# Attention, a gated layer and a soft mixture of experts on one core: sums joined on VectorE, more additions on VectorE, new due times, PSUM pairs in three pools, weights moved by 96 bytes

## The chip, the cores and the metric

The program runs on one core of a Trainium2 chip, as one launch. The metric is the device time of an execution in microseconds (us). A core has five engines that run their own instruction queues and meet at semaphores: PE (TensorE, matrix products into PSUM), DVE (VectorE), ACT (ScalarE), POOL (GpSimd), and SP (SyncE), which here issues all DMAs. A queue is executed in order: an instruction that waits holds up all that stand behind it.

## The reference

```python
def _attn_ref(q, k, v):                       # (4, 8, 1152, 64) each, fp32
    q_pool = q.reshape(B, H, S // 2, 2, D).mean(axis=3)
    scores = matmul(q_pool, k.transpose(0, 1, 3, 2)) / sqrt(D)
    scores = scores - max(scores, axis=-1)
    attn = exp(scores)
    attn = attn / (sum(attn, axis=-1) + 1e-09)
    return matmul(attn, v)

x = attention, laid out as (2304, 512)
h = x @ w_in                                  # (512, 2048)
x = (h * cos(h)) @ w_out                      # (2048, 512)

logits = x @ phi                              # 32 slots, 8 experts of 4 slots
slot_input = softmax(logits, over tokens).T @ x
slot_out[e] = relu(slot_input[e] @ w1[e]) @ w2[e]
return softmax(logits, over slots) @ slot_out
```

## The kernel before

**Three stages** follow one another: attention (up to about 416 us of the profiled execution), the gated layer (to about 790 us), the experts and the output (to the end). The change is in attention, in the passage to the gated layer, and in where the gated layer's weights lie.

**Attention** runs over 16 pairs of heads. A pair has 576 pooled queries in two halves of 288, and such a half is called a unit here: 32 units of J = 9 steps, one step for 128 keys. A step is: `scores` on PE (L347 four fp32 products, which the trace shows as eight; L351 four bf16 products that subtract the maximum), `exp` on ACT (L356), `av` on PE (L364, the product with v into the tile `o`), and `add` (L374), which adds the step's exponentials to a partial sum, on POOL or on DVE by the string `ADD_BY`. Before, "GGVGGVGGV" gives six steps to POOL (five additions) and three to DVE (two additions). After the ninth step `finish` multiplies the partial sums by ones on PE (`sums`, L431), which sums over the keys: one pass for the partial sum of POOL, one for that of DVE. Then `sums_out` on ACT (L438), four small DMAs (`fold`, L445), `total` on POOL (L449), `inv` on DVE (L453), DMAs `row` (L458) and `spread` (L462), `scale` on POOL (L465), and `store`, the split of the result into a high and a low part on ACT (L479) and POOL (L477). `take` (ACT, L417) and `join` (DVE, L421) read `o`.

**The maximum** of a pair's scores is found ahead of it: 14 rounds of a bf16 product on PE (`round_`, L274), each with a maximum over 768 columns on DVE (`reduce`, L279); `by_head` (PE, L286), `top` (DVE, L293 and L298) and `diagonal` (ACT, L305) make of them the tile D that L351 uses.

**PSUM** has 16 KB a partition. Attention uses three pairs of banks of 4 KB (`BANKS`, tags s0 to s2 of one pool `a_ps`) for scores, rounds and sums alike, and a fourth for `o`. The gated layer's pools `ps_h` and `ps_o` take over that memory.

**The order** is made by the class `Plan`. Every operation has an engine, a time that it is thought to take, what it follows, the ring buffers that it takes, and a due time. `Plan.order` goes forward in planned time and takes the operation that can start first; among those of one engine that can start at once, it takes the one that is due first. The plan lets no operation of POOL run beside an operation of DVE that is marked `port`. The due times are multiples of P, the planned time of a step. The instructions are then written out in that order, with semaphores from the data; nothing waits for a planned time.

**The gated layer** has 8 chunks of 256 of the 2048 columns, and 5 blocks of tokens (four of 512, one of 256). `gate` makes a product with w_in (L684, named hps), then its cosine in turns of ACT and DVE (L699 to L719) and a low part on POOL (L722); `project` multiplies with w_out (L684, named ops). Each product is three of fp32r: high by high, high by low, low by high. The first block of the first chunk (`first_gates`) is still planned with attention and takes one of its three PSUM pairs. The weights w come as 64-bit numbers and are decoded (L620 to L650) into high and low tiles: for even chunks into the pool `wts0`, which is allocated from the right end of SBUF, for odd chunks into `wts1i` and `wts1o` on the left. As built, the tiles of `wts0` start at bytes such as 202,720, which is 32 past a multiple of 64; those of `wts1i` and `wts1o` start at multiples of 128.

## Time and profile before

| | us |
|---|---|
| three runs | 918.54, 914.24, 917.77 (median 917.77) |
| the profiled execution | 914.82 |
| its span, first to last instruction | 912.9 |
| to the first scores | 17.9 |
| pairs 0 to 14, from the first scores of each | 374.5 |
| the last pair, to its last product in a row | 23.5 |
| from there to the second block's products in a steady row | 23.4 |
| gated layer to 790 us | 350.7 |
| the rest | 122.1 |

The page of the profile gives busy time and counts per engine, 40 slices of the span, the chain of work that ended last, and the costliest groups. The rows further down come from it and from answers of the trace. In a row by line and shape stand: line, engine, operation, output<-inputs, shapes, count | busy us, mean ns of one | idle time of the engine just before, with what ended it. A row of the timeline has the start, the time from start to end, and the instruction; "x8" is a run of eight. The time of one instruction on DVE or ACT includes the tail in which its writes land, and the next instruction can start inside it.

### The profile page before, as it was taken

How to read it: one execution, taken by the hardware profiler on the slowest of the kernel's cores; microseconds unless marked ns; L12 is line 12 of the kernel's file. 1: busy time of each engine (PE TensorE's matmuls, PEld its weight loads, DVE VectorE, ACT ScalarE, POOL GpSimd, SP SyncE). 2: the span in 40 equal slices, each digit the busy share in tenths (PEclk: the TensorE clock that was granted, in tenths of full speed). 3: DMA queues.
4: the chain of work that ended last, by engine and by line, in shares of the span. 5: the costliest groups of instructions: out<-in, count | busy, mean ns of one | idle time of the engine just before them, and what ended most of it. 6: DMA issues, size and time to landing. Idle time of an engine off the chain costs nothing.

```text
span 912.9 us, 24964 instructions
## 1 busy us (share of the span) xinstructions
PE 877.0 (96%) x10181; PEld 650.7 (71%) x10181; DVE 691.0 (76%) x1261; ACT 546.9 (60%) x1150; POOL 455.0 (50%) x445
## 2 busy tenths in 40 slices
PE   5999999899999999997999999999999999999997
PEld 2667766666666656765888888888888888777555
DVE  5778888787887878743899998888989887545524
ACT  3777777677777766674686554555555555445224
POOL 0677777776877767785444334334333343211000
PEclk9999999999999999998999999999999999999998
DMA  4133232333333332112111111111111110754797
GB/s 156 57 109 105 70 110 76 103 97 110 108 96 83 94 109 91 46 20 54 49 51 47 47 45 36 36 47 39 57 35 47 36 47 12 320 233 185 281 420 246
DMA packets 61363, 91.53 MB, mean 100 GB/s; under 512 B 29120, under 2 KB 40896, under 8 KB 57152
## 3 DMA queue, kind: packets, MB, share of 16 engines
q1 hardware_dynamic: 61248, 89.93, 30.5%
q8 instruction: 80, 1.31, 0.6%
q14 instruction: 35, 0.29, 0.1%
HBM read 78.71 MB, written 4.72 MB: 91 GB/s over the span
## 4 chain that ended last, share of the span: by engine, by line
PE 85%; DVE 5%; DMA 3%; ACT 3%; SPq 1%; issue 1%; POOL 0%; DVEq 0%; ACTq 0%; POOLq 0%
PE hps L684 21%; PE ops L684 20%; PE s L347 13%; PE o L364 13%; PE s L351 3%; PE m L274 3%; PE sums L431 3%; DVE mp L279 2%; PE hq L1225 2%; PE so L1268 2%; DVE r L702 1%; DMA kr<-in_k_dram 1%; DMA r<-row 1%; ACT r L709 1%; DMA qr<-in_q_dram 1%
## 5 line engine op out<-in xcount | busy, mean ns | idle before, releaser
L279 DVE TENSOR_REDUCE mp<-m 128x2 f32<-128x768 f32 x224 | 211.3, 951 | 56.8 <-PE m L274 56.2
L356 ACT ACTIVATE e<-s 128x576 f32<-128x576 f32 x288 | 184.1, 650 | 82.9 <-PE s L351 78.3
L684 PE MATMUL hps<-x,w 128*128 128x512 f32 (+1 forms) x960 | 211.9, 375 | 6.3 <-DVE r L712 6.3
L374 POOL TENSOR_TENSOR acc<-acc,e 128x576 f32<-128x576 f32 x128 | 185.4, 1449 | 64.0 <-ACT e L356 61.6
L684 PE MATMUL ops<-w,g 128*128 128x512 f32 x864 | 206.7, 393 | 0.0
L684 PEld LDWEIGHTS hps<-x,w 128*128 128x128 f32 x960 | 169.5, 190 | 41.8 <-DVE r L712 6.8
L347 PE MATMUL s<-qs,kr 64*64 64x288 f32 x2304 | 196.6, 408 | 2.8 <-ACT e L356 1.7
L364 PE MATMUL o<-e,vr 64*64 64x288 f32 x2304 | 190.1, 403 | 0.0
L684 PEld LDWEIGHTS ops<-w,g 128*128 128x128 f32 x864 | 161.5, 188 | 36.5 <-issue 0.6
L722 POOL TENSOR_TENSOR g<-r,g 128x512 fp32r<-128x512 f32 (+1 forms) x80 | 100.6, 1258 | 156.4 <-ACT g L719 120.7
L709 ACT ACTIVATE r<-r 128x512 f32<-128x512 f32 (+1 forms) x160 | 94.0, 587 | 76.2 <-DVE r L702 74.7
L347 PEld LDWEIGHTS s<-qs,kr 64*64 64x64 f32 x2304 | 89.5, 134 | 42.9 <-ACT e L356 4.8
L647 POOL TENSOR_TENSOR da<-da,w 128x256 f32<-128x256 f32 x64 | 51.1, 799 | 104.9 <-DVE db L636 43.6
L364 PEld LDWEIGHTS o<-e,vr 64*64 64x64 f32 x2304 | 87.4, 133 | 20.7
L274 PE MATMUL m<-kb,qb 64*64 64x384 bf16 x896 | 81.0, 335 | 14.1 <-ACT kb L234 5.7
L351 PE MATMUL s<-D,a_ones 64*64 64x288 bf16 x1152 | 90.7, 284 | 0.0
L702 DVE SCALAR_TENSOR_TENSOR r<-ki,hps 128x512 f32<-128x512 int32 (+1 forms) x80 | 50.3, 629 | 40.1 <-ACT ki L699 38.2
L699 ACT ACTIVATE ki<-hps 128x512 int32<-128x512 f32 (+1 forms) x80 | 44.1, 551 | 50.9 <-PE hps L684 50.6
L719 ACT CAST g<-r 128x512 fp32r<-128x512 f32 (+1 forms) x80 | 46.1, 577 | 41.4 <-DVE r L712 41.3
L374 POOL TENSOR_TENSOR acc<-e 128x576 f32<-128x576 f32 x32 | 46.5, 1455 | 44.1 <-ACT e L356 43.6
L835 DVE TENSOR_TENSOR acc<-acc,ops 128x512 f32<-128x512 f32 x70 | 47.3, 682 | 21.3 <-PE ops L684 21.2
L274 PEld LDWEIGHTS <-qb 64*64 64x64 bf16 x896 | 32.4, 108 | 39.2 <-issue 10.9
(146 smaller groups left out, 1005.4 us busy)
## 6 DMA issues: line engine op xcount, KB each, us to landing
raw<-in_w_io_dram SPq DMA_DIRECT2D x64, 256.0 KB
w1t<-in_w_dram SPq DMA_DIRECT2D x15, 1024.0 KB
vr<-in_v_dram SPq DMA_DIRECT2D x16, 576.0 KB
qr<-in_q_dram SPq DMA_DIRECT2D x15, 576.0 KB
kr<-in_k_dram SPq DMA_DIRECT2D x15, 576.0 KB
w2t<-in_w2b_dram SPq DMA_DIRECT2D x8, 1024.0 KB
r<-row SPq DMA_DIRECT2D x32, 144.0 KB
late<-in_w2a_dram SPq DMA_DIRECT2D x4, 1024.0 KB
```

Of the source, the lines that this page charges most:

```text
L274: nc.tensor.matmul(ps[heads[c], h.start // 64, 0:self.KC], w, m, start=True, stop=True)
L279: nc.vector.tensor_reduce(out=self.mp[p][:, x], in_=st[i][:, :, 0:self.KC], axis=AX.X, op=ALU.max)
L347: nc.tensor.matmul(ps[y:y + 64, h, 0:N], w, self.qs[p][x, s], start=True, stop=False)
L351: nc.tensor.matmul(ps[y:y + 64, h, 0:N], self.ones16[x], D[x, s], start=False, stop=True)
L356: nc.scalar.activation(out=st["e"], in_=st["ps"][:, :, 0:N], func=ACTF.Exp, scale=1.0 / 16.0)
L364: nc.tensor.matmul(self.o[u][64 * h:64 * h + 64, r, 0:N], self.vr[p][x, h, t], st["e"][x, h], start=(t == 0), stop=(t == J - 1),)
L374: eng.tensor_tensor(out=acc[who], in0=x, in1=st["e"], op=ALU.add)
L647: nc.gpsimd.tensor_tensor(out=st["a"], in0=st["a"], in1=fl(half(0)), op=ALU.subtract)
L684: nc.tensor.matmul(ps, x, y, start=(i == 0 and m == 0), stop=(i == n - 1 and m == 2))
L702: nc.vector.scalar_tensor_tensor(out=st["r"], in0=st["ki"], scalar=-c, in1=x, op0=ALU.mult, op1=ALU.add)
L709: nc.scalar.activation(out=st["r"], in_=st["r"], **kw)
L722: nc.gpsimd.tensor_tensor(out=g["l"][:, i], in0=st["r"], in1=fl(g["h"][:, i]), op=ALU.subtract)
```

## The change

1. `JOIN_BY = "V"`: DVE adds its partial sum to POOL's (`join_sums`, 128 x 2 x 288 fp32), and `sums` is one pass over one operand where it was two.
2. `ADD_BY` is "VVVVGGGGV": four additions on DVE and three on POOL in a unit, where it was two and five. `scale` and the low part of `store` stay on POOL.
3. The due times of attention become a table `DUES` with new values, with new values of P, `ROUNDS`, `BEHIND` and the first weights' times; the times in which loads are thought to land are longer; the first gates follow the decoding of the first weights. Only the order on the engines comes from these.
4. The three PSUM pairs become three pools of one buffer, and they are placed by which pair is used last, the earliest at the bottom.
5. A tile `edge` of 96 bytes is allocated at the right end ahead of `dec` and `wts0`. The tiles of `wts0` then start at 202,624 and the like, multiples of 128.
6. `consts` is written under the hand-made order as well.

```diff
-    P = 1.31
+    P = 1.3
-    ADD_BY = "GGVGGVGGV"
+    ADD_BY = "VVVVGGGGV"
-    BEHIND = 3.5
+    BEHIND = 6.36
+    DUES = {
+        "load": -0.1, "free": 4.8, "v": 10.9, "pooled": -16.1, "qb": 9.0, "kb": -8.9, "top": -21.5,
...
+    JOIN_BY, SCALE_BY, LOW_BY = "V", "G", "G"
+    HOLD = 3
...
-        self.ps_s = pool("a_ps", 1, space=PSUM)
+        self.ps_s = [pool(f"a_ps{i}", 1, space=PSUM) for i in range(self.BANKS)]
...
     def bank(self, key, name):
-        i = self.plan.slot[key]
-        return self.ps_s.tile([128, 2, 512], FP32, tag=f"s{i}", name=name)
+        return self.ps_s[self.place[self.plan.slot[key]]].tile([128, 2, 512], FP32, tag="s", name=name)
...
+        def join_sums():
+            self.engine(self.JOIN_BY).tensor_tensor(out=acc["G"], in0=acc["G"], in1=acc["V"], op=ALU.add)
+            del acc["V"]
...
-            x = op(s + 2 * P, who, (0.667, 1.37)[who == "G"],
+            x = op(s + due["add"] * P, who, (0.667, 1.37)[who == "G"],
...
+        if self.JOIN_BY:
+            x = op(s + due["whole"] * P, self.JOIN_BY, (0.667, 1.37)[self.JOIN_BY == "G"], join_sums,
+                   [where["G"][2], where["V"][2]], uses=[("aG", u), ("aV", u)], port=True)
+            where = {"G": (0, 0, x)}
         self.finish(p, c, avs[-1], [(x, (f"a{who}", u)) for who, (_, _, x) in where.items()] + whole, acc)
...
-        t = op(s + 3 * P, "P", 0.485 * len(adds), sums, [i for i, _ in adds], new=[("s", self.BANKS, ("sums", u))],
+        t = op(due("sums"), "P", 0.485 * len(adds), sums, [i for i, _ in adds], new=[("s", self.BANKS, ("sums", u))],
...
+        left = {}
+        for key, slot in plan.slot.items():
+            if plan.sizes_of[key] == "s":
+                left[slot] = max(left.get(slot, 0.0), *(start[i] for i in plan.users[key]))
+        self.place = {x: i for i, x in enumerate(sorted(left, key=left.get))}
...
-FIRST_FROM, FIRST_EVERY = 2, 1.6
+FIRST_FROM, FIRST_EVERY, FIRST_DUE = 2.68, 1.75, 159.1
...
+    edge = pool(ctx, "edge", 1, side="right").tile([128, 24], FP32, name="edge")
+    nc.vector.memset(edge, 0.0)
...
-            x = last[-2:] + done[:1]
+            x = last[-2:] + decoded + done[:1]
```

**VectorE in the middle of attention.** The rows are about one unit in the sixth pair before (mp<-m is a maximum, acc an addition of exponentials, mc the top, fold the inverse, xu the joining of `o`):

```order
L279 TENSOR_REDUCE mp<-m 128x2
L374 TENSOR_TENSOR acc<-e 128x576
L279 TENSOR_REDUCE mp<-m 128x2
L453 RECIPROCAL fold<-fold 128x36
L279 TENSOR_REDUCE mp<-m 128x2 x2
L421 TENSOR_TENSOR xu<-xu,o 128x288
L279 TENSOR_REDUCE mp<-m 128x2 x2
L374 TENSOR_TENSOR acc<-acc,e 128x576
L293 TENSOR_REDUCE mc<-m 128x4
```

And after, one unit at the like place (acc<-acc is the joining of the partial sums; da is a piece of the decoding):

```order
L388 TENSOR_TENSOR acc<-acc,e 128x576
L443 TENSOR_TENSOR xu<-xu,o 128x288
L391 TENSOR_TENSOR acc<-acc 128x576
L657 TENSOR_SCALAR da<-da 128x256
L388 TENSOR_TENSOR acc<-e 128x576
L660 TENSOR_SCALAR da<-da 128x256
L388 TENSOR_TENSOR acc<-acc,e 128x576
L665 SCALAR_TENSOR_TENSOR da<-raw,da 128x256
L388 TENSOR_TENSOR acc<-acc,e 128x576
L294 TENSOR_REDUCE mp<-m 128x2 x2
L475 RECIPROCAL fold<-fold 128x36
L294 TENSOR_REDUCE mp<-m 128x2 x2
```

Before, the additions stand singly between maxima; after, the unit's last addition, the joining and three additions of the next unit stand together, and the maxima follow together.

**ScalarE at the same places**, where e<-s is the exponential of a step. Before:

```order
L356 ACTIVATE e<-s 128x576 x2
L438 ACTIVATE r_3412<-sums 128x576
L305 ACTIVATE D<-a_minus,mc 128x64 x5
L356 ACTIVATE e<-s 128x576 x2
L479 CAST x_68<-xu 128x160
L479 CAST x_70<-xu 128x128
L644 CAST w<-da 128x256
L234 CAST qb<-qs 128x576
L356 ACTIVATE e<-s 128x576
L234 CAST kb<-kr 128x384
```

After:

```order
L320 ACTIVATE D<-a_minus,mc 128x64 x4
L460 ACTIVATE r_3266<-sums 128x576
L439 COPY xu<-o 128x288
L371 ACTIVATE e<-s 128x576 x8
L503 CAST x_68<-xu 128x288
L371 ACTIVATE e<-s 128x576
L320 ACTIVATE D<-a_minus,mc 128x64 x5
```

The exponentials of a unit, spread between other work before, now follow one another, seven or eight in a row; on PE the scores do so too, seven steps of a unit in a row ahead of its first product with v.

**TensorE at the end of attention**, with what a row waits for (hps<-x_66 is the first block's gate product, hps<-x_68 the second block's). Before:

```order
L684 MATMUL hps<-x_66,w 128x512
L431 MATMUL sums<-acc,a_ones 64x288 [waits PE_49,Pool_49]
L431 MATMUL sums<-acc,a_ones 64x288 x3
L431 MATMUL sums<-acc,a_ones 64x288 [waits DVE_49]
L431 MATMUL sums<-acc,a_ones 64x288 x3
L364 MATMUL o<-e,vr 64x288 [waits Activation_49]
L364 MATMUL o<-e,vr 64x288 x3
L684 MATMUL hps<-x_68,w 128x512 [waits DVE_49]
L684 MATMUL hps<-x_69,w 128x512
```

After:

```order
L379 MATMUL o<-e,vr 64x288 x4
L453 MATMUL sums<-acc,a_ones 64x288 [waits PE_49]
L453 MATMUL sums<-acc,a_ones 64x288 x3
L379 MATMUL o<-e,vr 64x288 x12
L453 MATMUL sums<-acc,a_ones 64x288 [waits DVE_49,PE_49]
L453 MATMUL sums<-acc,a_ones 64x288 x3
L720 MATMUL hps<-x_68,w 128x512 [waits Activation_49]
L720 MATMUL hps<-x_69,w 128x512 [waits Pool_49]
```

The second block's product waited for the last DVE instruction that reads the first block's products, since both lay in the lowest pair of banks; after, the first block's products lie in the highest of the three pairs, and the second block's first product waits for the ACT instruction that reads the sums of the last unit but one. The sums of the last two units stand close together there, and two gate products of the first block lie between products with v.

## Rows read from the trace of the kernel before

**Rows 1.** The page: busy by engine; the chain that ended last; exponentials.

```profile
PE 877.0 (96%) x10181; PEld 650.7 (71%) x10181; DVE 691.0 (76%) x1261; ACT 546.9 (60%) x1150; POOL 455.0 (50%) x445
...
PE 85%; DVE 5%; DMA 3%; ACT 3%; SPq 1%; issue 1%; POOL 0%; DVEq 0%; ACTq 0%; POOLq 0%
...
L356 ACT ACTIVATE e<-s 128x576 f32<-128x576 f32 x288 | 184.1, 650 | 82.9 <-PE s L351 78.3
```

**Rows 2.** Windows: length, busy of PE, PEld, DVE, ACT, POOL, clock, DMA, GB/s.

```profile
17.90:392.40 374.50, 365.90 (x6908) 253.28 (x6912) 300.13 (x433) 270.14 (x578) 276.87 (x253) 1.00 0.31 90
392.40:415.90 23.50, 23.50 (x440) 15.30 (x432) 10.62 (x15) 16.29 (x31) 19.52 (x19) 1.00 0.14 31
415.90:439.30 23.40, 17.14 (x83) 12.87 (x80) 9.29 (x19) 10.04 (x23) 8.78 (x11) 0.85 0.17 39
439.30:790.00 350.70, 350.70 (x1601) 289.13 (x1600) 306.48 (x650) 199.48 (x411) 136.75 (x145) 1.00 0.17 51
```

**Rows 3.** Groups by line and shape in 17.9 to 392.4 us.

```profile
L431 PE MATMUL sums<-acc,a_ones 64*64 64x288 f32 x464 | 33.9, 406 | 2.5 <-ACT e L356 1.4 <-DVE mp L279 0.8
...
L279 DVE TENSOR_REDUCE mp<-m 128x2 f32<-128x768 f32 x208 | 196.8, 951 | 55.1 <-PE m L274 54.5
L374 DVE TENSOR_TENSOR acc<-e 128x576 f32<-128x576 f32 x30 | 27.7, 924 | 0.3 <-ACT e L356 0.3
L374 DVE TENSOR_TENSOR acc<-acc,e 128x576 f32<-128x576 f32 x29 | 25.5, 881 | 0.0
...
L374 POOL TENSOR_TENSOR acc<-acc,e 128x576 f32<-128x576 f32 x119 | 172.2, 1447 | 60.7 <-ACT e L356 58.5
L374 POOL TENSOR_TENSOR acc<-e 128x576 f32<-128x576 f32 x30 | 43.7, 1458 | 43.9 <-ACT e L356 43.6
```

**Rows 4.** The chain of work in order of time, 405 to 450 us: start, length.

```profile
407.51 0.97 PE sums L431 x16
408.48 0.48 PE s L347 x8
408.97 0.12 PE s L351 x4
409.09 0.48 PE o L364 x8
```

**Rows 5.** Timeline of DVE and POOL: start, length, instruction.

```profile
8.98 7.01 DVE L279 TENSOR_REDUCE mp<-m 128x2 f32<-128x768 f32 x8
...
195.64 0.75 DVE L374 TENSOR_TENSOR acc<-acc,e 128x576 f32<-128x576 f32 x1
196.31 0.95 DVE L279 TENSOR_REDUCE mp<-m 128x2 f32<-128x768 f32 x1
...
414.94 1.41 POOL L374 TENSOR_TENSOR acc<-acc,e 128x576 f32<-128x576 f32 x1
...
415.34 1.63 DVE L374 TENSOR_TENSOR acc<-acc,e 128x576 f32<-128x576 f32 x1
```

**Rows 6.** The chain as in Rows 4, 180 to 192 us: a round.

```profile
188.35 0.16 PE m L274 x4
```

**Rows 7.** Timeline of PE at the end of attention.

```profile
421.75 1.20 PE L431 MATMUL sums<-acc,a_ones 64*64 64x288 f32 x16
422.77 0.66 PE L364 MATMUL o<-e,vr 64*64 64x288 f32 x8
429.70 8.33 PE L684 MATMUL hps<-x,w 128*128 128x512 f32 x24 [6.26 <-DVE r L712]
```

**Rows 8.** A window there, columns as in Rows 2.

```profile
429.70:435.10 5.40, 5.40 (x13) 4.24 (x14) 0.38 (x1) 0.60 (x1) 1.52 (x2) 0.50 0.11 20
```

**Rows 9.** Groups by shape on PE, weights of chunk 2: from 516.9 and 556.0 us.

```profile
L684 PE MATMUL hps<-x,w 128*128 128x512 f32 x24 | 5.8, 396 | 0.0
...
L684 PE MATMUL ops<-w,g 128*128 128x512 f32 x24 | 5.8, 396 | 0.0
```

**Rows 10.** The same, weights of chunk 1: from 489.5 and 494.9 us.

```profile
L684 PE MATMUL hps<-x,w 128*128 128x512 f32 x24 | 5.6, 389 | 0.0
...
L684 PE MATMUL ops<-w,g 128*128 128x512 f32 x24 | 5.6, 389 | 0.0
```

More of the change, by code (lines that the diff above doesn't have):

```diff
@@ L122 @@
 class Attention:
-    P = 1.31
+    P = 1.3
     QB, KC = 64, 384
-    ADD_BY = "GGVGGVGGV"
-    ROUNDS = (-13, -12, -11, -10, -9, -8, -7, -5, -3, -1, 1, 2, 3, 4)
+    ADD_BY = "VVVVGGGGV"
+    ROUNDS = (-25.8, -10.9, -8.3, -7.5, -7.4, -2.2, -1.9, -1.2, -11.3, -1.0, 0.7, 2.1, 2.3, 7.3)
     E_BUFS = 8
-    BEHIND = 3.5
+    BEHIND = 6.36
+    DUES = {
+        "load": -0.1, "free": 4.8, "v": 10.9, "pooled": -16.1, "qb": 9.0, "kb": -8.9, "top": -21.5,
+        "diagonal": 24.6, "add": 6.3, "whole": -15.1, "take": -13.8, "join": 10.2, "sums": 12.6, "out": -38.0,
+        "fold": -4.5, "total": 9.9, "inv": -17.4, "row": 34.5, "spread": 14.1, "scale": 0.9, "high": 29.2,
+        "low": -0.3,
+    }
+    JOIN_BY, SCALE_BY, LOW_BY = "V", "G", "G"
     BANKS = 3
+    HOLD = 3
     def __init__(self, ctx, tc, q, k, v, xt):
@@ L206, in operands @@
         k = k.rearrange("h d s -> (h d) s")
-        early = 0.0 if p == 0 else max(m + 12.0, 9.0)
+        at_ = lambda name, n=0.0: m + self.DUES[name] * self.P + n
+        early = 0.0 if p == 0 else max(at_("free"), 9.0)
         at = lambda parts: [(sum(parts[:i]), n) for i, n in enumerate(parts)]
@@ L482, in finish @@
         s = ((2 * p + c) * self.J + self.J - 1) * P
+        due = lambda name: s + self.DUES[name] * P
         x, r2, f, ro, rr = (("xu", u), ("r2", u), ("fold", u), ("row", u), ("r", u))
-        o1 = op(s + 2 * P, "A", 0.3, take, [last], new=[("xu", 4, x)], uses=[("o", u)])
-        o2 = op(s + 2 * P, "V", 0.36, join, [o1, last], uses=[x, ("o", u)])
-        t = op(s + 3 * P, "P", 0.485 * len(adds), sums, [i for i, _ in adds], new=[("s", self.BANKS, ("sums", u))],
+        o1 = op(due("take"), "A", 0.3, take, [last], new=[("xu", 4, x)], uses=[("o", u)])
@@ L487, in finish @@
+        o2 = op(due("join"), "V", 0.36, join, [o1, last], uses=[x, ("o", u)])
+        t = op(due("sums"), "P", 0.485 * len(adds), sums, [i for i, _ in adds], new=[("s", self.BANKS, ("sums", u))],
                uses=[k for _, k in adds])
-        t = op(s + 3.3 * P, "A", 0.547, sums_out, [t], new=[("r2", 2, r2)], uses=[("sums", u)])
+        t = op(due("out"), "A", 0.547, sums_out, [t], new=[("r2", 2, r2)], uses=[("sums", u)])
         self.rest = len(plan.ops)
-        t = op(s + 5 * P, "SP", 2.4, fold, [t], new=[("fold", 4, f)], uses=[r2], more=2.6)
@@ L491, in finish @@
-        t = op(s + 9 * P, "G", 0.22, total, [t], uses=[f])
-        t = op(s + 9 * P, "V", 0.29, inv, [t], uses=[f])
-        t = op(s + 9.5 * P, "SP", 1.3, row, [t], new=[("row", 4, ro)], uses=[f], more=2.6)
-        t = op(s + 11 * P, "SP", 0.6, spread, [t], new=[("r", 2, rr)], uses=[ro], more=3.0)
-        t = op(s + 13 * P, "G", 0.75, scale, [t, o2], uses=[x, rr])
-        t = op(s + 14 * P, "A", 0.34, lambda: store(False), [t], uses=[x])
-        op(s + 15 * P, "G", 0.75, lambda: store(True), [t], uses=[x])
+        t = op(due("fold"), "SP", 2.4, fold, [t], new=[("fold", 4, f)], uses=[r2], more=2.8)
@@ new lines, in finish @@
+        t = op(due("total"), "G", 0.22, total, [t], uses=[f])
+        t = op(due("inv"), "V", 0.29, inv, [t], uses=[f])
+        t = op(due("row"), "SP", 1.3, row, [t], new=[("row", 4, ro)], uses=[f], more=2.6)
+        t = op(due("spread"), "SP", 0.6, spread, [t], new=[("r", 2, rr)], uses=[ro], more=4.5)
+        t = op(due("scale"), self.SCALE_BY, (0.36, 0.755)[self.SCALE_BY == "G"], scale, [t, o2], uses=[x, rr], port=True)
+        t = op(due("high"), "A", 0.34, lambda: store(False), [t], uses=[x])
@@ L498, in finish @@
+        op(due("low"), self.LOW_BY, (0.36, 0.757)[self.LOW_BY == "G"], lambda: store(True), [t], uses=[x], port=True)
         self.rest = range(self.rest, len(plan.ops))
@@ L502, in run @@
         pair = 2 * J * P
-        self.q_after, self.k_after, self.s_after, self.v_after, self.D_after = {}, {}, {}, {}, {}
+        self.q_after, self.k_after, self.s_after, self.v_after, self.D_after, self.reds = {}, {}, {}, {}, {}, {}
         plan = self.plan
         for p in range(self.NP):
-            self.operands(p, (p - 1) * pair + 0.5 * P if p else -100.0)
+            self.operands(p, (p - 1) * pair + self.DUES["load"] * P if p else -100.0)
             self.maximum(p)
@@ L660, in read_part @@
         op = lambda j, after, **kw: plan.op(due, *steps[j][:2], steps[j][3], after, port=steps[j][2], **kw)
-        x = op(0, [], new=[("raw", 3, ("raw", k))], more=3.0, early=early)
+        x = op(0, [], new=[("raw", 3, ("raw", k))], more=4.6, early=early)
         x = op(1, [x], new=[("da", 2, ("da", k)), ("db", 2, ("db", k))], uses=[("raw", k)])
```

49 lines of the change are left out of this document (28 added, 21 removed).

## The prediction

> **What bounds the kernel now.** I read the page first: PE is busy for 96% of the span and is 85% of the chain that ended last [rows 1]. A busy PE can still be a waiting kernel, so I cut the span into its stages [rows 2]. In the 15 pairs from 17.9 to 392.4 us PE works 365.9 of 374.5 us, DVE 300.1 and POOL 276.9; so PE sets the pace there, with 8.6 us of idle time. DVE is not the limit: 54.5 us of the idle time ahead of its maxima are waits for PE [rows 3]. From 415.9 to 439.3 us PE stands still for 6.3 of 23.4 us, and its granted clock is 0.85 in the mean [rows 2]. From 439.3 to 790 us PE has no gap at all. So an edit pays if it takes work off PE, closes the hole at 424 to 430 us, or makes the products shorter; and it may cost nothing on DVE only as long as DVE stays under PE's time. I make the sum against the profiled execution, 914.82 us with a span of 912.9; the median of the runs, 917.77, is 0.3% above it.
>
> **Part 1, sums of one operand.** The chain gives 0.97 us for a unit's 16 products of `sums`, 0.48 + 0.12 for the scores of a step and 0.48 for its product with v [rows 4]. One pass of two goes, so 0.485 us of PE in each of 32 units: 15.5 us. Of these 29 units lie in the 15 pairs (464 products, 16 a unit [rows 3]): 14.1 us; two in the last pair, where PE is full [rows 2]: 1.0; one behind it: 0.5.
>
> **Part 2, more additions on DVE.** A unit gets two additions and one joining more, a pair six, 15 pairs 90. The price of one: from 195.64 to the next start at 196.31 is 0.67 us [rows 5]; a row's 0.75 holds a tail in which the next can start. That is 60 us, so DVE goes from 300.1 to 360 us if nothing else changes, while PE falls to 365.9 - 14.1 = 351.8. DVE becomes as long as PE, and this decides the case. Against the 360: eight maxima in a row take 7.01 us, (7.01 - 0.95) / 7 = 0.866 each [rows 5], where a row's mean is 0.951 [rows 3]; so 0.085 us of each counts as busy only where nothing follows at once. Were that so behind all 208 maxima, it would be 17.7 us; I take some half, 8 us, which vanish when DVE has no holes, and that leaves 352. The additions now take (27.7 + 25.5) / 59 = 0.90 us in the mean [rows 3], 0.15 above the undisturbed 0.75: they wait for POOL at times, as at 415.34, where one took 1.63 us while POOL added from 414.94 [rows 5]. POOL's own additions fall from 149 (119 + 30 [rows 3]) to 90, so that is no dearer per addition.
>
> What both engines do in a unit: PE has seven scores in a row, 7 x 0.6 = 4.2 us, while DVE does the five additions of its second fence and the one of `o`, 5 x 0.67 + 0.36 = 3.7 us; then PE alternates nine products with v, two scores, seven rounds of 0.16 [rows 6] and the sums, 9 x 0.48 + 1.2 + 1.1 + 0.5 = 7.1 us, while DVE takes seven maxima, 6.1 us, with the top, an inverse and half an addition of inputs, an estimated 0.8 more. Each phase has some 0.2 to 0.5 us of room on DVE, and less where a piece of decoding falls in. So the two interlock well but not wholly. I take 357.5 us for the 15 pairs, 23.8 a pair, which is PE's 351.8 with two thirds of today's 8.6 us of idle time. That is a gain of 17.0 (14.1 of it the sums, 2.9 from waits). The ends: PE alone, 351.8, a gain of 22.7; and DVE's 360 with handoffs as large as PE's now, 8.6, so 368.6, a gain of 6.
>
> **Part 3, due times and table values.** They add no instruction. What they move is in the order: exponentials in bursts, and `sums` late, so that its operand is ready. The SP queue keeps its DMAs in number and kind; loads still stand a pair ahead. I price this at nothing beside the 17.0; its cover is the three PSUM pairs: a burst needs a pair again after three scores, 1.8 us, and a score of 0.6 with an exponential of 0.65 [rows 1] and two handoffs frees it in less.
>
> **Part 4, PSUM in three pools.** The second block's products start at 429.70, 6.26 us after PE's last work, when the last DVE instruction that reads the first block's products has ended [rows 7]. Behind this hole the clock is granted at 0.50, the 1.2 GHz level, and 13 products take 5.40 us [rows 8]; products with weights of the same pool otherwise follow each other in (5.8 - 0.4) / 23 = 0.235 us [rows 9], and 13 would take 3.1. Hole and slow clock cost 6.3 + 2.3 = 8.6 us. After, the second block waits only for ACT's reading of the sums of the unit before last. PE's queue then has `sums` of the last unit ahead of it, which waits for the joining on DVE, which waits for POOL's last addition; between the last scores and that pass lie nine products with v, one of the sums and 24 gate products, 10 x 0.48 + 24 x 0.235 = 10.4 us, which is ample for three POOL additions of 1.45. The second gate product of the first block now waits for the first's reading on ACT, some 0.5 us. I take 7.5 of the 8.6; the ends are 3 (a new wait of some 3 us, behind which the clock falls again as it did) and 8.6.
>
> **Part 5, aligned weights.** In chunk 1, with weights in the left pools, 24 products take 5.6 us at 389 ns each [rows 10]; in chunk 2, with weights in `wts0`, 5.8 us at 396 ns, both where the weights are held (hps) and where they stream (ops) [rows 9]. The change goes to and fro with the pool through all chunks. So each product with a tile of `wts0` costs 7 ns more. There are 4 even chunks with 96 hps products of 512 columns and 108 ops products: 816 x 7 ns = 5.7 us, all on PE, which has no gap there. `wts0` starts 32 bytes past a multiple of 64, the others at multiples of 128; the shift makes them alike. I take the whole 5.7; the low end is 0, if the cause is the side of the memory and not the offset. DVE is at 306 of 350.7 us [rows 2] and hides behind PE.
>
> The Trainium skill's page "SBUF — State Buffer", section "Specifications (TRN2)", names 16-byte lines as what a read's rate depends on. By that rule 32 bytes past a multiple of 64 is as good a start as any, part 5 would give 0, and the time would be rival (b)'s; the trace has 7 ns between the pools and does not say by itself why.
>
> **The sum.** 17.0 + 1.0 + 0.5 + 7.5 + 5.7 = 31.7 us, so 914.8 - 31.7 = 883. The expert stage starts its loads when buffers come free and moves along with PE. As a median may stand a little above a profiled execution, I say 884.
>
> **Rivals.** (a) DVE becomes the bound in attention: 368.6 us for the 15 pairs, the gain of part 2 is 6 and not 17, and the time 895. For it: 360 against 352. Against it: DVE's tails and its waits for PE are in the 360. (b) The offset is not the cause: 884 + 5.7 = 890. Against it: rows 9 and 10 differ in nothing else that I see. (c) Part 4 does not do what it says, as another wait takes the hole's place (the decoding, or the joining behind POOL): 8 us back, 892. (d) Slower: POOL blocks DVE. Eight additions and two joinings a pair, each with two inputs in SBUF, could each meet a POOL addition of 1.45 us [rows 3]. If half of one is waited for, 0.7 us, that is 0.55 above today's 0.15 for each of ten: 5.5 us a pair on DVE's 24.0. The 15 pairs take 442, and the time is 968. It turns the change into a loss from 389 us, 25.9 a pair, or a mean block of about 0.35 us. Against it: POOL's additions of a unit use steps 5 to 8, DVE's steps 1 to 4, so they fall in different phases, and POOL adds 40% less.
>
> The Trainium skill's page "SBUF — State Buffer", section "Who interferes with whom", says that a DVE instruction with two SBUF inputs contends with a GpSimd instruction that reads SBUF, and that the loser waits for the whole instruction. The 1.63 us at 415.34 agrees [rows 5]; by this rule (d) is possible, and only the order keeps it off.
>
> **How the numbers follow.** As forecast 0.55 (876 to 889); (a) 0.18; (b) 0.10; (c) 0.07; (d) 0.05; and nothing won, as the parts eat each other, 0.05. The low end: 22.7 + 1.5 + 8.6 + 5.7 = 38.5, so 876, and 2 less for the spread of runs: 874. The high end holds (a) together with a part of (b), 895 + 5.7 = 901. A measurement can tell about 0.5%, 4.6 us, from no change. Faster by that: 0.55 + 0.18 + 0.10 + 0.07 = 0.90; within it 0.05; slower 0.05.
>
> **What would show it.** Part 1: 256 `sums` products instead of 512. Part 2: the first scores of the last pair come near 375 us; PE's idle time there is below 8 us; (a) would show maxima of DVE as what PE waits for, over 10 us in total, (d) additions with a mean over 1 us. Part 4: no gap of 6 us before the second block's products, and clock 1.00 through the passage. Part 5: 389 ns in all chunks; (b) would leave 396 in the even ones. The forecast is wrong if the 15 pairs take over 368 us, or if the passage keeps a gap over 3 us.

## The result: 4.1% faster, and where the 35 us came from

The changed kernel takes 879.69 us in the median of four runs (877.16 to 880.68), the kernel before 916.77 beside it; the ratio is 0.9593, with a 95% interval of 0.9561 to 0.9625. The prediction was 884. In the profiled executions the span goes from 912.9 to 877.6 us, 35.3 less. The page of the kernel after, as in [rows 1]: busy time, and the chain by engine (PEld is the weight load, which runs ahead of its product beside PE).

```profile
PE 850.7 (97%) x9925; PEld 629.2 (72%) x9925; DVE 735.4 (84%) x1358; ACT 541.6 (62%) x1150; POOL 358.5 (41%) x381
...
PE 81%; DVE 10%; ACT 4%; issue 2%; DMA 2%; SPq 1%; POOL 0%; DVEq 0%; ACTq 0%; POOLq 0%
```

To book the difference I cut both spans at the same points of the work: the first scores; the first scores of the last pair; the third block's first product; the first product of chunk 1; that of chunk 7; the last product of the gated layer. Windows of the kernel after, columns as in [rows 2]:

```profile
17.50:370.60 353.10, 350.33 (x6712) 236.29 (x6716) 339.58 (x521) 265.52 (x579) 188.39 (x192) 1.00 0.33 92
370.60:407.52 36.92, 35.07 (x454) 24.00 (x447) 21.26 (x32) 23.09 (x45) 19.97 (x22) 1.00 0.17 37
407.52:436.94 29.42, 28.09 (x134) 22.89 (x132) 28.34 (x55) 22.46 (x50) 15.20 (x16) 1.00 0.21 56
436.94:733.14 296.20, 296.20 (x1376) 248.12 (x1374) 266.61 (x582) 169.98 (x351) 117.07 (x129) 1.00 0.16 44
```

And of the kernel before, from the last pair on (the 15 pairs stand in [rows 2]):

```profile
392.40:439.29 46.89, 40.62 (x519) 28.16 (x511) 19.90 (x33) 26.32 (x53) 28.30 (x29) 0.93 0.16 35
439.29:467.37 28.08, 28.08 (x133) 23.17 (x132) 25.72 (x50) 21.88 (x47) 14.90 (x14) 1.00 0.20 57
467.37:768.37 301.00, 301.00 (x1375) 248.32 (x1374) 267.60 (x578) 168.50 (x347) 116.84 (x126) 1.00 0.15 42
```

| stretch | before | after | won | in the prediction's sum |
|---|---|---|---|---|
| 15 pairs | 374.5 | 353.1 | 21.4 | 17.0 |
| last pair and passage | 46.9 | 36.9 | 10.0 | 1.0 + 0.5 + 7.5 |
| rest of chunk 0 | 28.1 | 29.4 | -1.3 | part of the 5.7 |
| chunks 1 to 6 | 301.0 | 296.2 | 4.8 | part of the 5.7 |
| all else | 162.4 | 162.0 | 0.4 | 0 |

"All else" is what lies ahead of the first scores, chunk 7, and the experts with the output. (In the table of the time before, "the rest" is 912.9 - 790.0 = 122.9 us, not 122.1.)

The cut between the first two rows is not quite even. At the first scores of the last pair the kernel before still has 24 products with v and 12 of the rounds' products more ahead of it than the kernel after, some 3 x 0.48 + 3 x 0.16 = 1.9 us of TensorE. So about 1.9 of the 10.0 us belong to the 15 pairs.

**A yardstick for attention.** After, the scores of the fourth to seventh pair begin at 88.88, 112.00, 135.11 and 158.23 us: three pairs of 23.12 us each, in which TensorE never waits.

```profile
88.88:112.00 23.12, 23.12 (x453) 15.56 (x449) 22.56 (x38) 17.99 (x40) 12.77 (x14) 1.00 0.37 109
112.00:135.11 23.11, 23.11 (x452) 15.56 (x448) 22.00 (x36) 17.86 (x40) 12.49 (x13) 1.00 0.34 97
135.11:158.23 23.12, 23.12 (x453) 15.56 (x448) 22.56 (x38) 18.32 (x41) 12.77 (x14) 1.00 0.37 108
```

I take that as a pair's work, 346.8 us for 15 (and 14.1 more with two passes of the sums, 360.9). What a kernel takes beyond that in its 15 pairs is called lost below. Before it was 374.5 - 360.9 = 13.6 us (15.5 with the uneven cut), after 353.1 - 346.8 = 6.3. So TensorE's 8.6 us of idle time [rows 2] told only a part of what was lost. One profiled execution tells "lost" to some 3 us: three variants below whose attention is that of the change (PSUM pairs by number, no `edge`, `edge` of 32 bytes) take 353.0, 355.8 and 352.1 us in their 15 pairs, where the change takes 353.1.

**Of the 6.3 us, two pairs hold 3.4.** The seventh and the fourteenth take 24.80 us. The timelines of the kernel after in the seventh, of VectorE, of GpSimd and of TensorE:

```profile
172.69 0.95 DVE L673 SCALAR_TENSOR_TENSOR db<-raw,db 128x256 f32<-128x256 uint32 x1
173.57 3.46 DVE L388 TENSOR_TENSOR acc<-acc,e 128x576 f32<-128x576 f32 x2
176.95 1.81 DVE L294 TENSOR_REDUCE mp<-m 128x2 f32<-128x768 f32 x2
```

```profile
172.19 1.18 POOL L681 TENSOR_TENSOR da<-da,w 128x256 f32<-128x256 f32 x1 [2.70 <-DVE db L670]
173.33 0.98 POOL L487 TENSOR_TENSOR xu<-xu,r 128x288 f32<-128x288 f32 x1
174.27 0.77 POOL L471 TENSOR_TENSOR fold<-fold 128x36 f32<-128x36 f32 x1
175.00 1.40 POOL L388 TENSOR_TENSOR acc<-e 128x576 f32<-128x576 f32 x1
```

```profile
177.95 0.36 PE L289 MATMUL m<-kb,qb 64*64 64x384 bf16 x4 [1.35 <-DVE mp L294]
```

Two additions on VectorE take 3.46 us, where 0.75 is the undisturbed price of one [rows 5], because GpSimd works beside them; GpSimd is late there since it waited 2.70 us for a piece of decoding. The maxima come late, and TensorE waits 1.35 us. This is rival (d) in two of 15 pairs. It does not come in every execution: with the pairs by number and with `edge` of 32 bytes the seventh pair takes 23.56 and 23.55 us (the fourteenth 24.79 in both). There `total` on GpSimd (L471) waits over 1 us for its DMA and starts later, and the same two additions take 2.2 us.

### The profile page after: what moved, and what is told of

The parts are those of the page before. It is cut to its first block, busy times and chain, and to the rows that moved or that the text cites. A ratio compares the mean times of both kernels' runs of the same rounds, so it can differ in the third digit from the quotient of the medians.

```text
span 877.6 us, 24511 instructions
## 1 busy us (share of the span) xinstructions
PE 850.7 (97%) x9925; PEld 629.2 (72%) x9925; DVE 735.4 (84%) x1358; ACT 541.6 (62%) x1150; POOL 358.5 (41%) x381
## 4 chain that ended last, share of the span: by engine, by line
PE 81%; DVE 10%; ACT 4%; issue 2%; DMA 2%; SPq 1%; POOL 0%; DVEq 0%; ACTq 0%; POOLq 0%
PE hps L720 20%; PE ops L720 19%; PE o L379 13%; PE s L362 13%; PE m L289 4%; PE s L366 3%; DVE mp L294 3%; DVE r L738 2%; PE hq L1262 2%; PE so L1305 2%; PE sums L453 1%; DMA kr<-in_k_dram 1%; DVE acc L388 1%; ACT r L745 1%; PE xtp L884 1%
## 5 line engine op out<-in xcount | busy, mean ns | idle before, releaser
L371 ACT ACTIVATE e<-s 128x576 f32<-128x576 f32 x288 | 176.3, 652 | 60.8 <-PE s L366 59.4
L294 DVE TENSOR_REDUCE mp<-m 128x2 f32<-128x768 f32 x224 | 203.0, 942 | 9.8 <-PE m L289 8.0
L720 PE MATMUL hps<-x,w 128*128 128x512 f32 (+1 forms) x960 | 207.1, 370 | 1.1 <-ACT r L460 0.8
L720 PE MATMUL ops<-w,g 128*128 128x512 f32 x864 | 204.4, 390 | 1.3 <-POOL g L758 1.3
L362 PE MATMUL s<-qs,kr 64*64 64x288 f32 x2304 | 183.3, 406 | 0.9 <-DVE mp L294 0.8
L379 PE MATMUL o<-e,vr 64*64 64x288 f32 x2304 | 181.2, 403 | 0.0
L362 PEld LDWEIGHTS s<-qs,kr 64*64 64x64 f32 x2304 | 82.9, 134 | 39.9 <-DVE mp L294 3.7
L388 POOL TENSOR_TENSOR acc<-acc,e 128x576 f32<-128x576 f32 x64 | 90.9, 1420 | 1.5
L289 PE MATMUL m<-kb,qb 64*64 64x384 bf16 x896 | 78.7, 336 | 12.3 <-DVE mp L294 6.1
L388 DVE TENSOR_TENSOR acc<-acc,e 128x576 f32<-128x576 f32 x96 | 78.5, 817 | 3.5 <-ACT e L371 0.7
L872 DVE TENSOR_TENSOR acc<-acc,ops 128x512 f32<-128x512 f32 x70 | 47.1, 681 | 17.9 <-PE ops L720 17.8
```

The costliest lines, as they stand in the source:

```text
L289: nc.tensor.matmul(ps[heads[c], h.start // 64, 0:self.KC], w, m, start=True, stop=True)
L294: nc.vector.tensor_reduce(out=self.mp[p][:, x], in_=st[i][:, :, 0:self.KC], axis=AX.X, op=ALU.max)
L362: nc.tensor.matmul(ps[y:y + 64, h, 0:N], w, self.qs[p][x, s], start=True, stop=False)
L371: nc.scalar.activation(out=st["e"], in_=st["ps"][:, :, 0:N], func=ACTF.Exp, scale=1.0 / 16.0)
L379: nc.tensor.matmul(self.o[u][64 * h:64 * h + 64, r, 0:N], self.vr[p][x, h, t], st["e"][x, h], start=(t == 0), stop=(t == J - 1),)
L388: self.engine(who).tensor_tensor(out=acc[who], in0=x, in1=st["e"], op=ALU.add)
```

## The experiments

All variants start from the changed kernel. "Lost" is the 15 pairs less 346.8 us, or less 360.9 with two passes. The variants ran in three sets, without the change beside them; the kernel before, which ran beside each, had 914.69 to 915.16 us there and 916.77 beside the change. So medians of a variant and of the change compare to about 2 us.

| kernel | median us | 15 pairs | lost |
|---|---|---|---|
| before | 916.77 | 374.5 | 13.6 |
| the change | 879.69 | 353.1 | 6.3 |
| old due times | 915.21 | 375.8 | 29.0 |
| new due times, old operations | 907.99 | 379.2 | 18.3 |
| two passes, no joining | 908.81 | 381.9 | 21.0 |
| joining on GpSimd | 904.27 | 372.0 | 25.2 |
| additions shared as before | 907.88 | 373.1 | 26.3 |
| additions by turns | 908.08 | 376.4 | 29.6 |
| decoding at other places | 878.95 | 352.1 | 5.3 |

**Old due times.** The variables of the order go back; all else of the change stays.

```diff
-    P = 1.3
+    P = 1.31
...
-    BEHIND = 6.36
+    BEHIND = 3.5
...
-        "load": -0.1, "free": 4.8, "v": 10.9, "pooled": -16.1, "qb": 9.0, "kb": -8.9, "top": -21.5,
...
+        "load": 0.5, "free": 9.16, "v": 7.63, "pooled": 3.82, "qb": 4.58, "kb": 4.96, "top": 0.0,
+        "diagonal": 0.0, "add": 2.0, "whole": 2.0, "take": 2.0, "join": 2.0, "sums": 3.0, "out": 3.3,
...
-FIRST_FROM, FIRST_EVERY, FIRST_DUE = 2.68, 1.75, 159.1
+FIRST_FROM, FIRST_EVERY, FIRST_DUE = 2, 1.6, 1000.0
```

(`ROUNDS` is the old row too. The joining is new, so its due time here, "whole", has no old value.)

> The due times, P, the rounds' times, BEHIND and the times of the first weights are those of the kernel before; the joining, the sharing of the additions, the PSUM pools and the aligned weights are those of the change. Theory of the prediction, the due times are worth nothing of their own beside a few us of waits: TensorE has 350 us of work in the 15 pairs and some 9 us of idle time, so 360 us there and 887 in all. Rival, the due times carry the change, since they put VectorE's additions into TensorE's scores and its maxima into the products: VectorE and TensorE fall out of step, the 15 pairs take 368 us or more, and the time is 895 or more.

The rival holds, and by more than it asked: 915.21 us, a ratio to the kernel before of 0.9998 (0.9980 to 1.0016). Without the new due times the other parts together win nothing. Both kernels have the same instructions, 9925 products on TensorE, 1358 on VectorE, 1150 on ScalarE and 381 on GpSimd; what differs is their order. The window of its 15 pairs, and waits in it (engine and what it issued, what it waited for: us, times, longest):

```profile
16.90:392.70 375.80, 363.50 (x6688) 227.72 (x6692) 338.43 (x485) 268.01 (x568) 189.84 (x186) 1.00 0.30 87
```

```profile
DVE mp L294 <- PE m L289: 26.5, 51, 2.1
PEld s L362 <- DVE mp L294: 14.0, 28, 0.8
PEld s L362 <- ACT e L371: 13.0, 34, 1.4
PEld o L379 <- DVE xu L443: 6.3, 17, 0.7
```

The same view of the changed kernel:

```profile
DVE mp L294 <- PE m L289: 6.5, 22, 0.8
PEld s L362 <- DVE mp L294: 3.7, 8, 1.4
PEld s L362 <- ACT e L371: 1.8, 6, 0.4
```

Scores wait for a PSUM pair, which a maximum or an exponential has to free; with the new due times these waits fall from 27.0 to 5.5 us. (A weight load can wait while TensorE still works on the product ahead of it, so not all of the 27.0 us is lost: all waits of the loads add up to some 48 us there, and 29.0 are lost.) VectorE waits for rounds in turn, 26.5 us against 6.5. With the old due times VectorE also decodes only two of the eight first pieces of weights inside the 15 pairs, where it did all eight before the change; the first gates follow the decoding, and the rest of it stands in VectorE's queue among their cosines. In the passage, which takes 51.7 us and so 14.8 more, the sums wait 1.9 us for the joining, and a hole of 11.1 us opens ahead of the first products with w_out. Waits of TensorE from 392.7 us on, with the old due times:

```profile
PE ops L720 <- DVE r L748: 11.1, 1, 11.1
PE sums L453 <- DVE acc L391: 1.9, 1, 1.9
```

**New due times, old operations.** The other corner: two passes, no joining, the old string.

```diff
-    ADD_BY = "VVVVGGGGV"
+    ADD_BY = "GGVGGVGGV"
...
-    JOIN_BY, SCALE_BY, LOW_BY = "V", "G", "G"
+    JOIN_BY, SCALE_BY, LOW_BY = "", "G", "G"
```

> The new due times with the old operations: two passes of the sums, no joining, and the additions shared out as `GGVGGVGGV`; PSUM pools and aligned weights as in the change. TensorE then has 346.8 + 14.1 = 360.9 us of work in the 15 pairs. Theory, the new due times are good for any set of operations: about 367 us there, 893 in all. Rival, due times and operations fit each other only as a pair, so that this gives no better than the kernel before: 374 us or more in the 15 pairs, 900 or more.

The rival again: 379.2 us in the 15 pairs, more than before the change. So the due times are no gain in attention by themselves either. (The whole kernel takes 907.99 us, a ratio to the kernel before of 0.9926, 0.9904 to 0.9949: it has the change's placing in PSUM and its aligned weights.) The four corners in the 15 pairs are 374.5 (neither), 375.8 (operations alone), 379.2 (due times alone) and 353.1 (both). What a table of due times made for the old operations would win was not tried, so only the 14.1 us of the pass are known to be the operations' own.

**One operation back at a time.** Each alone:

```diff
-    JOIN_BY, SCALE_BY, LOW_BY = "V", "G", "G"
+    JOIN_BY, SCALE_BY, LOW_BY = "", "G", "G"
```

for the sums in two passes, "G" in place of the first "V" for the joining on GpSimd, and for the sharing of the additions one of

```diff
-    ADD_BY = "VVVVGGGGV"
+    ADD_BY = "GGVGGVGGV"
```

and "VGVGVGVGV".

First the sums in two passes:

> Without the joining on VectorE: `sums` has two operands and two passes again, all else of the change stays. Theory, TensorE sets the pace of attention: 32 passes of 0.485 us come back, 15.5 us, so 895, and TensorE has little idle time in the 15 pairs. Rival, VectorE had become the bound: 30 joinings of 0.67 us, 20 us, go from it, and the time rises by much less than 15, to 885 or below.

Neither: +29 us. The 15 pairs have 14.1 us more work, as the theory had it, and lose 14.7 more, which neither had. The loads for scores wait 8.4 us for maxima and 6.2 for exponentials there, 14.6 against 5.5 in the change; why the order no longer fits was not traced further. Then the joining on GpSimd:

> The joining of the two partial sums goes to GpSimd instead of VectorE; its place in the order follows from the same due times. Theory, TensorE sets the pace and VectorE has just enough room: VectorE loses 29 joinings of 0.67 us and GpSimd gains 30 of about 1.4, with room for them, so the time is 880 within 4 us. Rival, additions of GpSimd block VectorE wherever they meet: more GpSimd additions make more such blocks, the mean addition on VectorE rises above 0.9 us, and the time is 890 or more.

904 us, the rival's side, and this one shows blocking plainly. Groups of the 15 pairs there, the first additions of a unit on VectorE and the joining on GpSimd:

```profile
L388 DVE TENSOR_TENSOR acc<-e 128x576 f32<-128x576 f32 x30 | 40.8, 1359 | 7.0 <-ACT e L371 7.0
...
L391 POOL TENSOR_TENSOR acc<-acc 128x576 f32<-128x576 f32 x29 | 44.9, 1549 | 81.1 <-DVE acc L388 81.1
```

In the changed kernel the groups are these:

```profile
L388 DVE TENSOR_TENSOR acc<-acc,e 128x576 f32<-128x576 f32 x89 | 71.3, 801 | 2.8
L388 DVE TENSOR_TENSOR acc<-e 128x576 f32<-128x576 f32 x30 | 23.1, 770 | 1.9 <-ACT e L371 1.8
L391 DVE TENSOR_TENSOR acc<-acc 128x576 f32<-128x576 f32 x29 | 22.6, 780 | 0.3 <-DVE xu L443 0.2
```

The joining on GpSimd starts as the unit's additions on VectorE end, mostly just when VectorE begins the next unit: 1359 ns in the mean for an addition that takes 770 otherwise. Two such meetings, from the timelines of GpSimd and VectorE there:

```profile
105.04 1.46 POOL L391 TENSOR_TENSOR acc<-acc 128x576 f32<-128x576 f32 x1 [2.66 <-DVE acc L388]
105.15 1.96 DVE L388 TENSOR_TENSOR acc<-e 128x576 f32<-128x576 f32 x1
...
240.69 1.42 POOL L391 TENSOR_TENSOR acc<-acc 128x576 f32<-128x576 f32 x1 [2.68 <-DVE acc L388]
241.50 1.22 DVE L388 TENSOR_TENSOR acc<-e 128x576 f32<-128x576 f32 x1 [0.59 <-ACT e L371]
```

One addition starts 0.11 us behind the joining and one 0.81 us, and they end 2.07 and 2.03 us after its start, 0.6 after its end. The Trainium skill's page "SBUF — State Buffer", section "Who interferes with whom", says that a VectorE instruction with two SBUF inputs contends with a GpSimd instruction that reads SBUF, and that the one that comes later waits for the whole of the other; these rows agree. VectorE is busy hardly longer, 342.7 us against 339.6, since the joinings have left it; but its maxima stand behind the longer additions, and the loads for scores wait 12.5 us for them, against 3.7.

Then the sharing of the additions, as before and by turns:

> The additions are shared out as before, `GGVGGVGGV`, five on GpSimd and two on VectorE in a unit, with the joining on VectorE and all other parts of the change. Theory, the single pass of the sums is what wins and the sharing only makes room: the time stays near 880, at most 888, with the sums as late as GpSimd's fifth addition. Rival, the sharing in two phases is what keeps VectorE free of GpSimd: additions alternate on both engines again, VectorE's mean addition goes to 0.9 us and the 15 pairs take over 365 us, the time over 892.

> The same counts as in the change, four additions on VectorE and three on GpSimd, but by turns: `VGVGVGVGV` instead of `VVVVGGGGV`. Theory, blocking is real and the separate phases hold it off: VectorE's mean addition rises from 0.79 us to about 1.0 or more, TensorE waits for maxima, and the 15 pairs take 365 us or more, the time 892 or more. Rival, the sharing into phases is of no weight, since the order keeps the two engines apart in planned time whatever the string: 880 within 4 us.

Both give 908 us. Shared out as before, the rival's times come, but its mean does not: the additions take 0.85 us, and it is the joining on VectorE that GpSimd's additions lengthen, from 780 to 1469 ns:

```profile
L391 DVE TENSOR_TENSOR acc<-acc 128x576 f32<-128x576 f32 x29 | 42.6, 1469 | 1.0
```

By turns, the counts are those of the change, so the string's order, with the order of instructions that follows from it, is worth 23 us in the 15 pairs. The theory's times hold, but the mechanism that I had named is only a part: the mean addition on VectorE is 0.85 us for the later ones and 0.95 for the first ones, not 1.0 for all; (0.846 - 0.801) x 89 + (0.952 - 0.770) x 30 = 9.5 us. What the other 14 us are was not traced.

```profile
L388 DVE TENSOR_TENSOR acc<-acc,e 128x576 f32<-128x576 f32 x89 | 75.3, 846 | 1.7 <-ACT e L371 1.7
L388 DVE TENSOR_TENSOR acc<-e 128x576 f32<-128x576 f32 x30 | 28.6, 952 | 2.5 <-ACT e L371 2.5
```

In these two kernels and with the joining on GpSimd the passage takes 6 to 11 us more as well: the first products with w_out wait 4.3 to 7.3 us for VectorE's work on the first block's cosines, as with the old due times.

**Is it durations or sequence?** Two kernels keep the old due times' instructions in their order and make one engine's additions short:

```diff
-            self.engine(who).tensor_tensor(out=acc[who], in0=x, in1=st["e"], op=ALU.add)
+            n = 36 if who == "V" and not new else N
+            self.engine(who).tensor_tensor(out=acc[who][:, :, 0:n], in0=x[:, :, 0:n], in1=st["e"][:, :, 0:n], op=ALU.add)
```

(and the joining alike; the other kernel has "G" in place of "V" in the condition, and the joining whole).

> The kernel with the old due times, its instructions in the same order, but three of VectorE's four additions in a unit and the joining go over 72 instead of 576 columns, so the sums leave most of these exponentials out. VectorE is freed of some 60 us in the 15 pairs, which took 375.8 us there. Theory, scores wait for PSUM because VectorE's additions stand between the maxima that free it: the 15 pairs fall to 355 us or less, the time to 895 or less. Rival, the sequence of scores, rounds and exponentials on TensorE and ScalarE makes the waits by itself: over 368 us and over 907.

> The kernel with the old due times, its instructions in the same order, but two of GpSimd's three additions in a unit go over 72 instead of 576 columns, so the sums leave most of these exponentials out. GpSimd is freed of some 70 us in the 15 pairs. Theory, GpSimd's additions block VectorE's and so lengthen the waits: VectorE's mean addition falls from 0.89 to under 0.8 us and the 15 pairs from 375.8 to 368 us or less. Rival, the blocking is a small part of it: 372 to 377 us.

VectorE's busy time falls from 338.4 to 278.8 us, and the 15 pairs only from 375.8 to 367.4; with GpSimd's short they take 371.6 (medians 906.80 and 911.08 us). So VectorE's length is some 8.4 of the 29.0 us lost, GpSimd's some 4.2 (and the two overlap: with GpSimd's short, VectorE is busy for 8.2 us less). The first theory fell short of its 355, and its rival's 368 was missed by 0.6; the second missed its 368, and its rival's 372 was missed by 0.4. The larger part, 20.6 us, stays where VectorE has much time to spare. Windows and waits with VectorE's additions short:

```profile
16.80:384.20 367.40, 359.18 (x6684) 229.17 (x6688) 278.82 (x485) 267.47 (x568) 179.54 (x187) 1.00 0.31 89
```

```profile
DVE mp L294 <- PE m L289: 50.3, 89, 2.6
PEld s L362 <- ACT e L371: 16.3, 38, 1.8
PEld s L362 <- DVE mp L294: 8.8, 17, 0.8
```

The waits for exponentials are not shorter than with full additions (16.3 against 13.0 us). What is left to make them is the sequence in which scores, rounds and exponentials use three PSUM pairs. That is concluded from what the short additions do not change, and not shown by a run of its own; which of the due times sets the sequence right was not tried one by one.

**The place in PSUM.** The pairs by number, as in the kernel before:

```diff
-        self.place = {x: i for i, x in enumerate(sorted(left, key=left.get))}
+        self.place = {x: i for i, x in enumerate(sorted(left))}
```

> The three PSUM pairs are placed by their number, as in the kernel before, instead of by their last use; so the first block's gate products lie at the bottom and the second block's first product waits for VectorE's last read of them. Theory, the place makes the hole: a gap of about 6 us before the second block's products with a low clock behind it, 6 to 8.6 us more, so 886 to 888. Rival, the passage is shorter for another reason (earlier gates, the decoding ahead of them): a gap under 3 us and at most 882.

Mechanism and time part here. The hole is back, with the low clock (0.52) behind it; timeline and window of this kernel, and then the timeline of the changed one:

```profile
403.92 8.10 PE L720 MATMUL hps<-x,w 128*128 128x512 f32 x24 [4.29 <-DVE r L748]
```

```profile
403.90:409.20 5.30, 5.28 (x13) 4.19 (x14) 0.76 (x2) 0.62 (x1) 2.22 (x4) 0.52 0.10 11
```

```profile
400.59 5.74 PE L720 MATMUL hps<-x,w 128*128 128x512 f32 x24 [0.77 <-ACT r L460]
...
421.84 0.50 PE L720 MATMUL ops<-w,g 128*128 128x512 f32 x1 [0.69 <-POOL g L758]
...
430.98 0.50 PE L720 MATMUL ops<-w,g 128*128 128x512 f32 x1 [0.64 <-POOL g L758]
```

From the last pair's first scores to the third block it takes 413.22 - 370.40 = 42.8 us against 36.9: 5.9 us for the placing. But the rest of chunk 0 takes 27.4 us there against 29.4, so 2.0 are given back. What gives them back are mostly the two waits at 421.84 and 430.98 us for `g`, 1.3 together, which exist only without the hole. VectorE is busy 28.34 of 29.42 us in that stretch (the window further up): it computes the cosines that g needs, and it starts this stretch with less done, 32 instructions and 21.3 us of work since the last pair's first scores, where it has done 36 and 23.1 with the hole. The hole's cover was thinner than the prediction had it.

The median is 881.96, 2.3 above the change, and this difference is not clear of noise: the ratios to the kernel before are 0.9631 (0.9612 to 0.9651) and 0.9593 (0.9561 to 0.9625). The profiled execution, at 884.67 us, is the slowest of four. Its mean granted clock is 0.989, that of the other three 0.994, as in the change; whether they have the low clock behind the hole is not on record.

**The alignment.** Without `edge`, which puts the tiles of `wts0` 96 bytes past a multiple of 128 again, and with 32 bytes, which puts them on odd multiples of 64:

```diff
-    edge = pool(ctx, "edge", 1, side="right").tile([128, 24], FP32, name="edge")
+    edge = pool(ctx, "edge", 1, side="right").tile([128, 8], FP32, name="edge")
```

> The changed kernel without the tile `edge`; the tiles of `wts0` start 32 bytes past a multiple of 64 again, all else is the same. Theory, the offset is the cause: the products of chunks 2, 4 and 6 take 396 ns again and those of chunks 1, 3 and 5 stay near 389; the time rises by 5 to 6 us, from 879.7 to about 885. Rival, the shift is not the cause and the time of a product moved by something else in the change: 389 ns in all chunks and 880.

> The tile `edge` has 32 bytes instead of 96, so the tiles of `wts0` start at odd multiples of 64. Theory, a multiple of 64 is enough: 389 ns in all chunks and 880. Rival, a multiple of 128 is wanted: 396 ns or something between in chunks 2, 4 and 6, and up to 885.

Without it the median is 886.03, 6.3 more. Groups by shape inside chunk 2, first without `edge`, then with 32 bytes, then with 96:

```profile
L718 PE MATMUL ops<-w,g 128*128 128x512 f32 x84 | 20.2, 394 | 0.0
L718 PE MATMUL hps<-x,w 128*128 128x512 f32 x61 | 14.7, 396 | 0.0
```

```profile
L720 PE MATMUL ops<-w,g 128*128 128x512 f32 x84 | 20.0, 393 | 0.0
L720 PE MATMUL hps<-x,w 128*128 128x512 f32 x61 | 14.7, 395 | 0.0
```

```profile
L720 PE MATMUL ops<-w,g 128*128 128x512 f32 x84 | 19.7, 389 | 0.0
L720 PE MATMUL hps<-x,w 128*128 128x512 f32 x60 | 14.1, 389 | 0.0
```

Products with weights of chunk 1, which `edge` does not move, keep their time without it:

```profile
L718 PE MATMUL ops<-w,g 128*128 128x512 f32 x24 | 5.6, 390 | 0.0
```

The offset is the cause, and a multiple of 64 is not enough. From chunk 1 to chunk 7 it takes 300.99 us without `edge`, 299.70 with 32 bytes and 296.20 with 96, the same in all eleven kernels here that have 96. (The time of the 32-byte kernel, 880.45 us, is one run and can't tell this; what lies ahead of chunk 1 and behind chunk 6 was 1.0 and 1.5 us shorter.) Of the 6.3 us between the medians only the 4.8 of these chunks are the products' for certain: without `edge` the profiled execution takes 2.7 us more in the 15 pairs, where the tile has no part.

**A version that might be better.** The decoding moved away from the place where it met the additions:

```diff
-FIRST_FROM, FIRST_EVERY, FIRST_DUE = 2.68, 1.75, 159.1
+FIRST_FROM, FIRST_EVERY, FIRST_DUE = 2.93, 1.5, 159.1
```

> The whole change, with the first weights' decoding at other places: from 2.93 pairs on, one every 1.5 pairs, where it was 2.68 and 1.75. In the seventh and the fourteenth pair of the changed kernel two VectorE additions took 3.46 us beside GpSimd's work, TensorE waited 1.35 us for a maximum, and these pairs took 24.8 us instead of 23.12; a piece of decoding stood just ahead in both. Theory, the decoding at this place of a pair pushes GpSimd's work into VectorE's additions: no pair over 24 us after the second, and 2 to 3.4 us less, about 877. Rival, such meetings come from elsewhere or turn up in other pairs: 880 within 2 us.

878.95 us (875.93 to 879.75) can't be told from 879.69, and the rival holds. The fourteenth pair, in which no piece of decoding stands among the additions any more, takes 23.17 us, which bears the reason out. But the seventh still takes 24.23, with a piece of decoding between its additions, and the tenth is new with 24.26. No version here beats the change.

## Why the prediction came out right

**The likeliest case held, with a gain of 35.3 us in the span for a forecast 31.7.** The forecast's own signs mostly came: 256 `sums` products, the last pair's first scores at 370.6 us (forecast 375), TensorE's idle time in the 15 pairs 353.10 - 350.33 = 2.8 us (below 8), 389 ns in all chunks from 1 to 6, clock 1.00 through the passage. That the sum came so near is in part luck: by its own terms it was 4.4 us short in the 15 pairs, 1.0 short in the passage and 2.2 too high in the gated layer (4.8 - 1.3 = 3.5 for 5.7), and one of its steps was wrong.

- **Part 1, sums: right.** TensorE's busy time in the 15 pairs falls by 365.9 - 350.3 = 15.6 us; 14.1 of it are the pass. The 1.5 above, and 1.9 more for the products that moved ahead of the cut, I put down to waits that had counted as busy.
- **Part 2, VectorE: right, with a reason of the wrong size and one that it lacked.** I had VectorE at 352 us; it is 339.6. The 89 additions and joinings more cost (71.3 + 23.1 + 22.6) - 53.2 = 63.8 us, so 0.72 each against my 0.67. Two things gave 24.3 back, where I had 8. Taken one by one (count times mean of every group of rows), VectorE's instructions in the 15 pairs add up to 321.4 us before and 374.4 after, so 21.3 and 34.8 us of that lie under the next instruction: the tails that vanish are 13.5 us and not 8. And what I had left alone got 10.8 us shorter: the addition of inputs goes from 911 to 746 ns, and three of the decoding steps from 473 to 501 down to 283. GpSimd is busy for 188.4 us beside them instead of 276.9; with the old sharing of the additions (274.6 us of GpSimd) the addition of inputs takes 1006 ns again and two of these steps 550 and 588. That is how VectorE stays under TensorE's time and rival (a) did not come.
- **The term of the 15 pairs was mis-sized: 17.0, and 21.4 came.** I took TensorE's idle time, 8.6 us, for all that was lost, and its busy time less the pass, 351.8, for its work. A pair's work is 23.12 us, so 346.8. What was lost was therefore 13.6: the rows of TensorE's products do not show all of it, and weight loads waited as well. That a product whose load waits counts as busy in part is my reading of this; no row shows it by itself.
- **Part 3 was the step that failed.** "I price this at nothing beside the 17.0": with the old due times, the 15 pairs take 22.7 us more and the passage 14.8 more, and the whole kernel is as slow as before. In the 15 pairs the fit of order and operations, not a sum of parts, made the gain. My sum came out because it took for granted an order in which both engines run on; I had read that from the rows of VectorE and ScalarE in the change, yet gave it no price, and none of my rivals was "the order doesn't fit". Rival (c) comes nearest: under the old due times the joining and the decoding take the hole's place, as it said, and the passage takes 14.8 us more where it had 8.
- **Part 4: right in place, too high in worth.** The gap of 6.26 us [rows 7] became one of 0.77, and the low clock [rows 8] is gone. The placing itself is 5.9 us in the profiled executions, of which 2.0 come back in chunk 0, mostly as waits for GpSimd behind VectorE. Of the other 4.1 of the passage's 10.0, 1.5 are the single pass and some 1.9 are the uneven cut; the hole is also shorter, 4.29 us for 6.26, with the first block's gates further ahead of attention's end. I had named the joining and the first gates as new waits, and not the cosines of the next blocks.
- **Part 5: right.** 396 became 389 ns, and it is worth 4.8 us in chunks 1 to 6, and 6.3 in the medians with and without `edge`, for a forecast 5.7. Rival (b) fell, as the tiles stayed on their side of the memory and only the offset moved; starts that are multiples of 16 and of 64 bytes were not enough.
- **Rival (d) is real but local.** It takes 3.4 us in two pairs here; with the joining on GpSimd it stretches a unit's first addition to 1.36 us in the mean, and the time rises by 25 us.

## What to carry to other kernels

An order that fits a set of operations is a part of that set: move, split or drop one operation and price the whole order anew. Each of the four edits of attention's operations cost 25 to 29 us here, where it put 15.5 us more work on TensorE at most, and the old due times cost 35; only moving the decoding was free. Read what a matrix engine has lost from a stretch that doesn't wait (its shortest period, repeated exactly), and not from its idle column alone. And where a hole closes, look which engine was catching up inside it: what it had not finished turns up as the next wait.
